# One product of 33 rows for the flags of masked rows, and a start, a router and a weight split that are issued in another order

## The chip, the cores and the metric

One core of one Trainium2 chip. The metric is the device time of one execution in microseconds (us); three runs of the kernel before are shown. TensorE is PE in the views, VectorE is DVE, ScalarE is ACT, GpSimd is POOL, and SP is the engine that only issues transfers (DMAs).

## What is computed

Attention with a bucket mask (a query sees the keys that fall into its own bucket of 64), then a layer that sends each token to the expert with the largest logit, then a two-layer block with a leaky activation, all in float32.

```python
scores = scale * np.matmul(q, k.transpose(0, 1, 3, 2))      # 16 heads, 768 x 768, width 64
scores = np.where(mask, scores, -1000000000.0)              # mask: same bucket
scores = scores - np.max(scores, axis=-1, keepdims=True)
attn = np.exp(scores)
attn = attn / (np.sum(attn, axis=-1, keepdims=True) + 1e-09)
x = np.matmul(attn, v)                                      # 1536 tokens x 512
h = np.maximum(x[tokens] @ w1[e], 0.0)                      # e: the token's expert of 8
y = gate_w * (h @ w2[e])
out = leaky(y @ w_in, alpha) @ w_out
```

A query whose bucket holds no key is a masked row: all its scores are equal, so its output is the mean of v over all keys.

## The kernel before

The 16 heads run as 96 slots, six slots of 128 keys for each head. In slot s PE makes the scores of 128 keys against 768 queries in two halves (ST, L823 and L824), ACT takes the exponential (L825) and its float16 part Eh (L829), POOL the rest El (L830), and four slots later PE multiplies both by v (AV, L838 to L840) into one accumulator `av`, of which there is one. NORM (L851 to L853, DVE) divides it and so frees it for the next head.

A masked row is found from the head's row maxima. MAX (L791 on PE, a reduction at L792 on DVE) computes them some slots ahead of use; POSTb (L797 to L804) transposes them, writes the row `mr` back into the head's operand tile OP by a transfer (L800), which the head's first ST waits for, and compares it with a threshold into the flags `ft`, which a second transfer (L804, for head 0 L814) lays out as one row FL of 768 float16 values. At the end of a head AV adds, for each of six column blocks, flag times total of v, as two products of one row each:

```python
mm(a[:,c*65:c*65+65],fc,VT[:,0,h%4],start=False,stop=False,skip_group_check=True)
mm(a[:,c*65:c*65+64],fc,VT[:,1,h%4,0:64],start=False,stop=(c==5),skip_group_check=True)
```

VT holds the total of v in two float16 parts (high and rest, written by DVE in vtot, L730 and L731). A head's operand tile OP is filled by transfers that SP issues one after another: the bucket bits `zb` (L618 from `big`), A (three transfers) and B (two), which are the float32r part of k and q and its rest; B is made by POOL (L677). `load` (L624, L625) brings k and q of one head.

What is issued when is written by hand: the loop over slots takes its steps in the order of the letters of ORDER, `at`, `sl_at` and `v_at` put a step into a slot, `later` collects transfers for the next flush, and the table PLAN holds slot numbers. `first` there lists the slots whose end runs one more step of the router for the first 768 tokens (some 60 small DVE instructions in all: S, R, star, star2 at L299 to L315, adjust at L324 to L340, its one-hot at L263, GATE at L222 to L228, pre at L350 to L356, gates at L271 to L275). `ga` lists the slots of three gathers of tokens on POOL, and `w1` those of the eight splits of the first expert's weights (L585 on ACT, L588 on DVE). `v0` places the scale of the first v heads: vscale2 (L709 on PE, L711 on DVE) is its last step.

The first microseconds are written out ahead of the loop: WARM idle products of 128x128 (L655), Z0 (bucket bits of heads 0 and 1), six MAX, mrow (L807, L808: the row maxima of head 0 by PE and DVE), six MAX, mrow, then the first ST. `clear` (L653, L654) zeroes one of the five OP tiles on POOL.

Of the kernel before, what the change touches and what calls it, by code (L numbers as in the profile page):

```python
# [9 lines left out]
F32 = mybir.dt.float32  # L10
# [14 lines left out]
NH = 16  # L25
# [11 lines left out]
ORDER = "aVDNmbnefopAL"  # L37
PM = 2
PLAN = dict(
    v0=(1, 2, 4), T3=(2, 2), Z3=(5, 6), T=(2, 4, 5, 7), Z=(8, 10), ld1=5, ld=0, am1=(9, 10, 11, 12), am=(4, 6, 8,  # L40
    10), sc=(13, 15), tot=3, tot0=6, sp=(-2, 4, 10, 18), cap=(3, 2, 0, 1), x=(1, 2, 7, 3), x3=(0, 1, 2, 2), x4=(9, 10, 13, 11), w1=(91, 92, 93, 94, 96, 97, 98, 99), ga=(78, 81, 84), vl=1, am0=(0, 0), Z2=(0, 1), x6=(0, 1, 6, 4), first=(57, 58, 59, 60, 62, 63, 64, 67, 71, 72, 73),
)
NPRE = 3
NT = 22
# [429 lines left out]
def _program(base, tc, nc, q, k, v, proj, mod, w_gate, mbias, w1, w2, win, wout, alpha, out):  # L474
# [142 lines left out]
    def f32(ap): return ap.bitcast(F32)  # L617
# [34 lines left out]
    def clear(i):  # L652
        nc.gpsimd.memset(f32(OP[i][64:128,1:3,:]),0.0)  # L653
        nc.gpsimd.memset(f32(OP[i][96:97,1,:]),1.0)  # L654
    for n in range(WARM): mm(pt[:,128:256],one,one,start=True,stop=True)  # L655
    p0h=ep.tile([128,44],F32R,tag="p0h",name="p0h"); p0l=ep.tile([128,44],F32R,tag="p0l",name="p0l")
    for t in (p0h,p0l): nc.vector.memset(f32(t),0.0)
# [18 lines left out]
        nc.scalar.activation(A[h],raw[h],AF.Copy)  # L676
        nc.gpsimd.tensor_tensor(out=B[h],in0=raw[h],in1=f32(A[h]),op=ALU.subtract)  # L677
    onesh=cp.tile([128,128],F16,tag="onesh",name="onesh")
    VT=cp.tile([1,2,4,65],F16,tag="vt",name="vt")
    FL=[cp.tile([1,768],F16,tag=f"fl{i}",name=f"fl{i}") for i in range(3)]  # L680
    VH=[cp.tile([128,6,4,65],F16,tag=f"vh{i}",name=f"vh{i}") for i in range(2)]
    VL=[cp.tile([128,6,4,64],F16,tag=f"vl{i}",name=f"vl{i}") for i in range(2)]
    DG=[cp.tile([128,4],F32,tag=f"dg{i}",name=f"dg{i}") for i in range(2)]
    def fill():
        for t in DG: nc.gpsimd.memset(t,0.0)
        nc.gpsimd.memset(onesh,2.0**-8)
        nc.gpsimd.memset(VT[:,0,:,64:65],3.0)
# [35 lines left out]
    def vtot(h):  # L723

        w,i=divmod(h,4)
        p=misc()
        for j in range(6):
            mm(p[:,0:64],onesh,VH[w%2][:,j,i,0:64],start=(j==0),stop=False)
            mm(p[:,0:64],onesh,VL[w%2][:,j,i,:],start=False,stop=(j==5))
        nc.vector.tensor_copy(VT[:,0,i,0:64],p[0:1,0:64])  # L730
        nc.vector.tensor_tensor(out=VT[:,1,i,0:64],in0=p[0:1,0:64],in1=VT[:,0,i,0:64],op=ALU.subtract)  # L731

    dq=[];todo=[];now=[True]
    def later(f,p):
        if now[0]: f()
        else: todo.append((p,f))
# [6 lines left out]
    def T(h,half):  # L743
        if half==0:
            half0(h)
        elif h>1:
            OD(h)
            if 4<h+3<NH: at(13,lambda:load(8)) if h==5 else later(lambda:load(h+3),2)
    def OD(h,ns=range(5)):
        t=OP[h%NP]; lo,hi=slice(0,64),slice(64,128)  # L750
        k2=A[h][lo].unsqueeze(1).to_broadcast([64,2,768])
# [25 lines left out]
    def Z0(h,half):  # L777
        p=misc()
        sl=slice(half*384,half*384+384)
        mm(p[0:44,0:384],p0h,A[h][:,sl],start=True,stop=False)  # L780
        mm(p[0:44,0:384],p0h,B[h][:,sl],start=False,stop=False)
        mm(p[0:44,0:384],p0l,A[h][:,sl],start=False,stop=True)
        for o_ in range(2):
            ps=slice(32*o_,32*o_+12)
            nc.vector.tensor_scalar(out=OP[h][64:76,1+o_,sl],in0=p[ps,0:384],scalar1=tv0[ps,0:1],scalar2=tv0[ps,1:2],op0=ALU.is_gt,op1=ALU.mult)
# [7 lines left out]
    def POSTa(h,c0=0,c1=6):  # L793
        nc.vector.tensor_reduce(out=mts[h%2][:,c0:c1],in_=mx[h][:,c0:c1],axis=AX.X,op=ALU.max)
    def POSTb(h,c0=0,c1=6):
        p=misc(); n=c1-c0
        nc.tensor.transpose(p[0:n,0:128],mts[h%2][:,c0:c1],ident)  # L797
        mr=wp.tile([6,128],F32R,tag="mr",name="mr")
        nc.vector.tensor_scalar(out=mr[0:n],in0=p[0:n,0:128],scalar1=MK,scalar2=-1.0,op0=ALU.max,op1=ALU.mult)
        nc.sync.dma_start(out=f32(OP[h%NP][96:97,2,c0*128:c1*128].rearrange("o (c p) -> o c p",p=128)),in_=f32(mr[0:n]))  # L800
        if h not in flT: flT[h]=FL[h%3]
        ft=wp.tile([6,128],F16,tag="ft",name="ft")
        nc.vector.tensor_scalar(out=ft[0:n],in0=p[0:n,0:128],scalar1=MK,scalar2=None,op0=ALU.is_lt)
        later(lambda f=flT[h]:nc.sync.dma_start(out=f[0:1,c0*128:c1*128].rearrange("r (c p) -> r c p",p=128),in_=ft[0:n]),1)  # L804
    def mrow(half):
        p=misc(); hs=slice(half*384,half*384+384)
        for c in range(3): nc.tensor.transpose(p[0:1,c*128:c*128+128],mts[0][:,3*half+c:3*half+c+1],ident)  # L807
        nc.vector.tensor_scalar(out=OP[0][96:97,2,hs],in0=p[0:1,0:384],scalar1=MK,scalar2=-1.0,op0=ALU.max,op1=ALU.mult)  # L808
    def flags0():
        p=misc()  # L810
        nc.tensor.transpose(p[0:6,0:128],mts[0],ident)
        ft=wp.tile([6,128],F16,tag="ft",name="ft"); flT[0]=FL[0]
        nc.vector.tensor_scalar(out=ft,in0=p[0:6,0:128],scalar1=MK,scalar2=None,op0=ALU.is_lt)
        later(lambda:nc.sync.dma_start(out=FL[0][0:1].rearrange("r (c p) -> r c p",p=128),in_=ft),1)  # L814
    E={}
    def ST(s,a):
        h,j=divmod(s,6); t=OP[h%NP]
# [14 lines left out]
    def AV(s):  # L832
        h,j=divmod(s,6); b,hh=divmod(h,8)
        if j==0: av[h]=ps1.tile([128,512],F32,tag="av",name="av")
        _,eh,el=E.pop(s); a=av[h]
        for c in range(6):
            cs=slice(c*128,c*128+128)
            mm(a[:,c*65:c*65+65],eh[:,cs],VH[h//4%2][:,j,h%4,:],start=(j==0 and c==0),stop=False,skip_group_check=True)  # L838
            mm(a[:,c*65:c*65+64],eh[:,cs],VL[h//4%2][:,j,h%4,:],start=False,stop=False,skip_group_check=True)  # L839
            mm(a[:,c*65:c*65+65],el[:,cs],VH[h//4%2][:,j,h%4,:],start=False,stop=False,skip_group_check=True)  # L840
        if j==5:
            for c in range(6):
                fc=flT[h][:,c*128:c*128+128]
                mm(a[:,c*65:c*65+65],fc,VT[:,0,h%4],start=False,stop=False,skip_group_check=True)
                mm(a[:,c*65:c*65+64],fc,VT[:,1,h%4,0:64],start=False,stop=(c==5),skip_group_check=True)
    def NORM(h):
        b,hh=divmod(h,8)
        if hh==0: xs[b]=xsv[b]
# [10 lines left out]
    def at(s,f): other.setdefault(s,[]).append(f)  # L859
    def sl_at(s,f): slot.setdefault(s,[]).append(f)  # L860
# [14 lines left out]
    fill()  # L875
    for u in range(3):
        for a in range(2): MAX(u,a)
    POSTa(0,0,3); mrow(0)
    for u in range(3,6):
        for a in range(2): MAX(u,a)  # L880
    POSTa(0,3,6)
    ahead=(0,1,2)
    Z0(1,0); ST(0,0)
    mrow(1); Z0(1,1); ST(1,0)
    for i in range(2): vam(0,slice(i,i+1))
    ST(2,0)
    direct(2); OD(1,(3,4)); load(3); OD(2,(1,3,4))
    at(1,lambda:load(4)); at(3,lambda:load(5)); sl_at(0,flags0); at(2,lambda:clear(4))
    for i in range(2): at(PLAN["am0"][i],lambda i=i:vam(0,slice(i+2,i+3)))
    for t in range(2): sl_at(PLAN["Z2"][t],lambda t=t:Z((2,),t))  # L890
    v_at(PLAN["v0"][2],0)
# [609 lines left out]
```

## Time and profile before

| what | us |
|---|---|
| median of 3 runs | 712.32 (711.87 to 714.47) |
| the profiled execution | 713.37, its span 711.6 |
| PE busy in the span | 676.3 (95%), 5032 products |
| DVE, ACT, POOL busy | 441.4, 332.9, 234.2 |
| mean granted clock of PE | 0.973 |

The views used below are: the busy time of the engines by stretches, with PE's granted clock (1.00 is 2.4 GHz, 0.50 is 1.2 GHz); the waits of PE; and the timelines of one engine, in which a row gives the start, the time of one instruction or of a merged run (x gives how many), and in brackets the idle time before it with what ended it.

### The profile page before, as it was taken

To read this page: it belongs to the slowest core of one execution; us is meant where nothing else is said; L and a number is where in the kernel's file an instruction comes from. 1 tells how busy PE (TensorE), PEld (TensorE's weight loads), DVE (VectorE), ACT (ScalarE), POOL (GpSimd) and SP (SyncE) were. 2 spreads that over 40 slices of the span, in tenths; PEclk is the share of its full clock that TensorE was granted. 3 is DMA by queue.
4 is the path that set the end of the run, shared out by engine and by line. 5 is a ranking of instruction groups with operands and counts; after the bars stand their busy time and mean duration, and the time that the engine had idled before them with its cause. 6 is when DMAs were issued, how large, how long until landed. Compare 5 with 4: busy or idle time off the path is not lost. (4 is left out here: it accounts for less than half of the span.)

```text
span 711.6 us, 13120 instructions
## 1 busy us (share of the span) xinstructions
PE 676.3 (95%) x5032; PEld 563.1 (79%) x5032; DVE 441.4 (62%) x905; ACT 332.9 (47%) x561; POOL 234.2 (33%) x204
## 2 busy tenths in 40 slices
PE   6789999999899989999999989999999999999996
PEld 5568998998779777788888777788888888888884
DVE  6867888889887668316723557999643344434332
ACT  5556887887677935225524337666311111111111
POOL 8367999898758400210100022021021010110002
PEclk8679999999999999999999999999999999999998
DMA  8267873874625141316622274433011010010001
GB/s 213 70 161 166 179 168 75 179 204 106 136 73 196 41 155 69 105 33 225 220 90 74 81 262 146 134 132 135 1 39 51 0 30 1 15 45 0 1 1 59
DMA packets 31229, 72.40 MB, mean 102 GB/s; under 512 B 6924, under 2 KB 7014, under 8 KB 30902
## 3 DMA queue, kind: packets, MB, share of 16 engines
q1 hardware_dynamic: 28068, 61.78, 30.6%
q0 software_dynamic: 2960, 9.70, 4.0%
q8 instruction: 41, 0.67, 0.4%
q14 instruction: 30, 0.25, 0.1%
q10 hardware_dynamic: 130, 0.00, 0.0%
HBM read 79.15 MB, written 12.06 MB: 128 GB/s over the span
## 5 line engine op out<-in xcount | busy, mean ns | idle before, releaser
L830 POOL TENSOR_TENSOR El<-E,Eh 128x768 f16<-128x768 f32 x88 | 144.3, 1652 | 43.4 <-ACT Eh L829 20.2
L825 ACT ACTIVATE E<-st 128x384 f32<-128x384 f32 x192 | 89.5, 493 | 59.9 <-PE st L824 55.8
L792 DVE TENSOR_REDUCE mx<-mxp 128x1 f32<-128x384 f32 x192 | 97.7, 547 | 10.7 <-PE mxp L791 10.3
L585 ACT ACTIVATE gh<-gf 128x512 fp32r<-128x512 f32 x48 | 30.2, 630 | 143.9 <-PE o L1346 133.4
L829 ACT ACTIVATE Eh<-E 128x768 f16<-128x768 f32 x94 | 79.5, 846 | 0.1
L823 PE MATMUL st<-op 97*128 97x384 f32 x192 | 74.8, 390 | 2.8 <-DMA op<-mr 2.5
L791 PE MATMUL mxp<-op 76*128 76x384 f32 x192 | 68.4, 372 | 5.3 <-DVE mx L792 2.0
L588 DVE TENSOR_TENSOR gl<-gf,gh 128x512 fp32r<-128x512 f32 x48 | 33.1, 690 | 60.0 <-ACT gh L585 57.9
L1048 PE MATMUL y<-op,hh 128*128 128x512 f32 x208 | 69.7, 402 | 0.2 <-DVEq L1257 0.2
L1320 PE MATMUL h<-big,op 128*128 128x512 f32 x256 | 68.5, 396 | 0.0
L824 PE MATMUL st<-op 128*128 128x384 f32 x192 | 67.6, 352 | 0.0
L1363 POOL DMA_INDIRECT out_dram<-x,did x12 | 11.8, 985 | 169.3 <-DVE x L1360 89.8
L1346 PE MATMUL o<-op,gh 128*128 128x512 f32 x192 | 64.2, 395 | 0.0
L1025 PE MATMUL g<-op,xh 128*128 128x512 f32 x192 | 62.6, 397 | 1.3 <-DVEq L1105 0.8
L838 PE MATMUL av<-vh,Eh 128*128 128x65 f16 x576 | 59.7, 198 | 3.7 <-DVE big L853 3.7
L838 PEld LDWEIGHTS <-Eh 128*128 128x128 f16 x576 | 53.1, 99 | 11.4 <-issue 6.8
L839 PE MATMUL av<-vl,Eh 128*128 128x64 f16 x576 | 59.2, 196 | 0.0
L840 PE MATMUL av<-vh,El 128*128 128x65 f16 x576 | 59.0, 196 | 0.0
L1320 PEld LDWEIGHTS h<-big,op 128*128 128x128 f32 x256 | 48.2, 188 | 11.5
L839 PEld LDWEIGHTS <-Eh 128*128 128x128 f16 x576 | 53.9, 100 | 0.1
L840 PEld LDWEIGHTS <-El 128*128 128x128 f16 x576 | 53.8, 99 | 0.0
L1202 POOL DMA_INDIRECT yg<-ys,dpos x10 | 12.4, 1243 | 120.8 <-DVE x L1156 64.6
(404 smaller groups left out, 1510.8 us busy)
## 6 DMA issues: line engine op xcount, KB each, us to landing
r<-in_moe_w_dram SPq DMA_DIRECT2D x42, 1024.0 KB
op<-B SPq DMA_DIRECT2D x32, 192.0 KB
op<-in_moe_w_in_dram SPq DMA_DIRECT2D x6, 1024.0 KB
op<-A SPq DMA_DIRECT2D x28, 192.0 KB
op<-A SPq DMA_DIRECT2D x13, 384.0 KB
op<-in_moe_w_out_dram SPq DMA_DIRECT2D x4, 1024.0 KB
ys<-ysb SPq DMA_DIRECT2D x13, 256.0 KB
big<-in_q_dram SPq DMA_DIRECT2D x17, 192.0 KB
```

The costliest lines, as they stand in the source:

```text
L791: mm(p[:,0:384],t[0:76,2,c*128:(c+1)*128],t[0:76,1,a*384:a*384+384],start=True,stop=True)
L792: nc.vector.tensor_reduce(out=mx[h][:,c,a:a+1],in_=p[:,0:384],axis=AX.X,op=ALU.max)
L823: mm(p[:,0:384],t[0:97,1,js],t[0:97,2,qs],start=True,stop=False)
L824: mm(p[:,0:384],t[:,0,js],t[:,3,qs],start=False,stop=True)
L825: nc.scalar.activation(E[s][0][:,qs],p[:,0:384],AF.Exp,scale=0.125)
L829: else: nc.scalar.activation(eh,e,AF.Copy)
L830: (nc.vector if s>=ELD else nc.gpsimd).tensor_tensor(out=el,in0=e,in1=eh,op=ALU.subtract)
L838: mm(a[:,c*65:c*65+65],eh[:,cs],VH[h//4%2][:,j,h%4,:],start=(j==0 and c==0),stop=False,skip_group_check=True)
L839: mm(a[:,c*65:c*65+64],eh[:,cs],VL[h//4%2][:,j,h%4,:],start=False,stop=False,skip_group_check=True)
L840: mm(a[:,c*65:c*65+65],el[:,cs],VH[h//4%2][:,j,h%4,:],start=False,stop=False,skip_group_check=True)
L1048: nc.tensor.matmul(yps[t], a[:, ks], b[:, kk], start=(kk == 0 and n == 0), stop=(kk == 7 and n == 2))
L1320: nc.tensor.matmul(p, terms[t][0][:, kk, cs], terms[t][1][:, kk], start=(n == 0), stop=(n == 11))
```

## The change

Flags and totals move into one product: VT becomes a tile of 33 rows with the high part of the total in row 0 and the rest in row 32, FL gets 33 rows, cleared once, with the flags in rows 0 and 32. So the flags are transferred twice (32 transfers where there were 16), and AV makes six products per head where it made twelve. In the start, 17 idle products are put in at four places, the loads of heads 4 and 5 are both issued in slot 0 (before: slots 1 and 3), the load of head 6 goes from slot 2's flush to slot 5, the fifth `clear` goes into `fill`, and vscale2 goes from slot 2 to slot 3. In the router star2 goes from slot 62 to 63, adjust from 63 to 71, its one-hot from 64 to 72, GATE from 67 to 75, pre from 71 and 72 to 80 and 81, gates from 73 to 83; the gathers go from slots 78, 81, 84 to 84, 85, 87; six of the eight splits of w1 go two or one slots later.

```diff
-    v0=(1, 2, 4), ...
+    v0=(1, 3, 4), ...
-    ... w1=(91, 92, 93, 94, 96, 97, 98, 99), ga=(78, 81, 84), ... first=(57, 58, 59, 60, 62, 63, 64, 67, 71, 72, 73),
+    ... w1=(91, 92, 95, 96, 97, 98, 99, 100), ga=(84, 85, 87), ... first=(57, 58, 59, 60, 63, 71, 72, 75, 80, 81, 83),
+    def idle(n):
+        p=ps1.tile([128,512],F32,tag="av",name="idle")
+        for _ in range(n): mm(p[:,0:128],one,one,start=True,stop=True)
-    VT=cp.tile([1,2,4,65],F16,tag="vt",name="vt")
-    FL=[cp.tile([1,768],F16,tag=f"fl{i}",name=f"fl{i}") for i in range(3)]
+    VT=cp.tile([33,4,65],F16,tag="vt",name="vt")
+    FL=[cp.tile([33,768],F16,tag=f"fl{i}",name=f"fl{i}") for i in range(3)]
     def fill():
-        nc.gpsimd.memset(VT[:,0,:,64:65],3.0)
+        nc.gpsimd.memset(VT[:,:,64:65],0.0)
+        nc.gpsimd.memset(VT[0:1,:,64:65],3.0)
+        for t in FL: nc.gpsimd.memset(t,0.0)
         clear(3)
+        clear(4)
     def vtot(h):
-        nc.vector.tensor_copy(VT[:,0,i,0:64],p[0:1,0:64])
-        nc.vector.tensor_tensor(out=VT[:,1,i,0:64],in0=p[0:1,0:64],in1=VT[:,0,i,0:64],op=ALU.subtract)
+        nc.vector.tensor_copy(VT[:,i,0:64],p[0:33,0:64])
+        nc.vector.tensor_tensor(out=VT[32:33,i,0:64],in0=p[32:33,0:64],in1=VT[32:33,i,0:64],op=ALU.subtract)
     def T(h,half):
-            if 4<h+3<NH: at(13,lambda:load(8)) if h==5 else later(lambda:load(h+3),2)
+            if 4<h+3<NH: at(13 if h==5 else 5,lambda:load(h+3)) if h in (3,5) else later(lambda:load(h+3),2)
     def POSTb(h,c0=0,c1=6):
-        later(lambda f=flT[h]:nc.sync.dma_start(out=f[0:1,...],in_=ft[0:n]),1)
+        for z in (0,32): later(lambda f=flT[h],z=z:nc.sync.dma_start(out=f[z:z+1,...],in_=ft[0:n]),1)
     def AV(s):
-                mm(a[:,c*65:c*65+65],fc,VT[:,0,h%4],start=False,stop=False,skip_group_check=True)
-                mm(a[:,c*65:c*65+64],fc,VT[:,1,h%4,0:64],start=False,stop=(c==5),skip_group_check=True)
+                mm(a[:,c*65:c*65+65],fc,VT[:,h%4],start=False,stop=(c==5),skip_group_check=True)
-    POSTa(0,0,3); mrow(0)
+    POSTa(0,0,3); idle(7); mrow(0)
     Z0(1,0); ST(0,0)
-    mrow(1); Z0(1,1); ST(1,0)
+    idle(2); mrow(1); idle(3); Z0(1,1); ST(1,0)
-    ST(2,0)
+    ST(2,0); idle(5)
-    at(1,lambda:load(4)); at(3,lambda:load(5)); sl_at(0,flags0); at(2,lambda:clear(4))
+    at(0,lambda:(load(4),load(5))); sl_at(0,flags0)
```

The issue order of SP in slots 0 to 4, where `op_140`, `op_141` and `op_142` are the operand tiles of heads 1, 2 and 3, `big_74` holds raw k and q and the bucket bits, and `fl` the flags. Before:

```order
L814 DMA fl_187<-ft 1x6x128
L624 DMA big_74<-in_k_dram 64x768
L625 DMA big_74<-in_q_dram 64x768
L618 DMA op_141<-big_74 12x768 x2
L618 DMA op_142<-A 64x2x768
L618 DMA op_142<-A 64x768 x2
L618 DMA op_142<-B 64x768 x2
L624 DMA big_74<-in_k_dram 64x768
L625 DMA big_74<-in_q_dram 64x768
L624 DMA big_74<-in_k_dram 64x768
L625 DMA big_74<-in_q_dram 64x768
L800 DMA op_140<-mr 1x6x128
```

And in the change (its line numbers are five or six higher there):

```order
L624 DMA big_74<-in_k_dram 64x768
L625 DMA big_74<-in_q_dram 64x768
L624 DMA big_74<-in_k_dram 64x768
L625 DMA big_74<-in_q_dram 64x768
L820 DMA fl_187<-ft 1x6x128 x2
L618 DMA op_141<-big_74 12x768 x2
L618 DMA op_142<-A 64x2x768
L618 DMA op_142<-A 64x768 x2
L618 DMA op_142<-B 64x768 x2
L806 DMA op_140<-mr 1x6x128
L810 DMA fl_188<-ft 1x6x128 x2
```

Between B of head 3 and `mr` of head 1 no load is left; one load moved ahead of the flags, one behind them.

The order of DVE around the NORM of slot 64 (`r<-av,sc` to `big_73<-av,r`). Before, the second half of adjust stands right ahead of it and the one-hot behind it:

```order
L337 TENSOR_SCALAR misc<-misc 128x6
L338 CAST rq<-misc 128x6
L339 CAST misc<-misc 128x6
L340 CAST rm<-misc 128x6
L851 TENSOR_SCALAR r<-av,sc 128x6
L852 RECIPROCAL r<-r 128x6
L853 TENSOR_TENSOR big_73<-av,r 128x6x64
L792 TENSOR_REDUCE mx<-mxp 128x1 x2
L263 TENSOR_TENSOR big_3223<-iota,misc 128x768
```

In the change star2 stands there, and the maxima follow without the one-hot:

```order
L309 TENSOR_SCALAR misc<-misc,es 128x8
L311 TENSOR_TENSOR so<-misc,iota 128x8
L312 COPY misc<-so 128x8
L315 TENSOR_TENSOR om<-misc,so 128x64
L856 TENSOR_SCALAR r<-av,sc 128x6
L857 RECIPROCAL r<-r 128x6
L858 TENSOR_TENSOR big_73<-av,r 128x6x64
L798 TENSOR_REDUCE mx<-mxp 128x1 x6
```

adjust moved from the slot ahead of this NORM to the slot behind the next one.

The order of PE in the start of the change; before, the three rows of L657 are not there:

```order
L797 MATMUL mxp<-op_139 128x384 x6
L657 MATMUL idle<-one 128x128 x7
L813 MATMUL misc<-ident,mt_181 1x128 x3
L797 MATMUL mxp<-op_139 128x384 x6
L786 MATMUL misc<-A,p0h 44x384
L787 MATMUL misc<-B,p0h 44x384
L788 MATMUL misc<-A,p0l 44x384
L829 MATMUL st<-op_139 128x384
L830 MATMUL st<-op_139 128x384
L657 MATMUL idle<-one 128x128 x2
L813 MATMUL misc<-ident,mt_181 1x128 x3
L657 MATMUL idle<-one 128x128 x3
```

The idle products stand ahead of transposes and products that wait for DVE; five more follow three products of the score, ahead of the maxima of head 1.

## Rows read from the trace of the kernel before

**Rows 1.** Waits of PE from 60 to 150 us: total, times, longest.

```profile
PE mxp L791 <- ACT E L825: 0.7, 1, 0.7
```

**Rows 2.** Timeline of PE at head 0's flags: start, time, product.

```profile
54.17 0.19 PE L839 MATMUL av<-vl,Eh 128*128 128x64 f16 x1
54.20 0.20 PE L840 MATMUL av<-vh,El 128*128 128x65 f16 x1
54.33 0.20 PE L844 MATMUL av<-vt,fl 1*128 1x65 f16 x1
...
54.67 0.19 PE L845 MATMUL av<-vt,fl 1*128 1x64 f16 x1
54.79 0.45 PE L823 MATMUL st<-op 97*128 97x384 f32 x1
```

**Rows 3.** Timeline of PE in the start.

```profile
2.65 4.21 PE L655 MATMUL misc<-one 128*128 128x128 f32 x18 [0.31 <-DVE p0h L657]
...
13.74 0.80 PE L807 MATMUL misc<-ident,mt 128*1 128x128 f32 x3 [1.92 <-DVE mt L794]
...
31.27 0.59 PE L709 MATMUL misc<-dg,one 128*128 128x4 f32 x2 [1.27 <-DVE dg L705]
...
44.36 0.41 PE L823 MATMUL st<-op 97*128 97x384 f32 x1 [2.46 <-DMA op<-mr]
```

**Rows 4.** Stretches: length, busy PE, PEld, DVE, ACT, POOL, clock, DMA share, GB/s.

```profile
10.00:14.00 4.00, 1.78 (x7) 0.97 (x8) 3.52 (x8) 3.32 (x4) 3.80 (x4) 0.58 0.94 209
...
24.00:31.00 7.00, 5.74 (x17) 3.60 (x17) 6.76 (x18) 2.75 (x5) 1.65 (x1) 0.52 0.12 34
31.00:41.00 10.00, 9.73 (x59) 9.23 (x60) 6.96 (x17) 7.12 (x13) 9.47 (x7) 0.50 0.69 172
...
44.00:48.00 4.00, 3.64 (x22) 2.87 (x23) 1.84 (x4) 1.71 (x3) 0.71 (x1) 0.60 0.43 169
```

**Rows 5.** Timeline of SP, 37 to 42 us: start and time of issue.

```profile
37.13 1.10 SPq L618 DMA_DIRECT2D op<-B  x2
...
40.90 0.78 SPq L800 DMA_DIRECT2D op<-mr  x1
41.78 0.73 SPq L804 DMA_DIRECT2D fl<-ft  x1
```

**Rows 6.** Timeline of DVE: the row `mr` of head 1.

```profile
38.26 0.27 DVE L799 TENSOR_SCALAR mr<-misc 6x128 fp32r<-6x128 f32 x1
```

**Rows 7.** Timeline of POOL, 33 to 37 us.

```profile
33.05 1.37 POOL L653 MEMSET op<- 64x1536 f32 x1
...
35.29 1.82 POOL L677 TENSOR_TENSOR B<-big,A 128x768 fp32r<-128x768 f32 x1
```

**Rows 8.** Timeline of DVE around the NORM of slot 64.

```profile
176.38 0.21 DVE L299 TENSOR_SCALAR misc<-k,es 128x8 f32<-128x8 f32 x1
...
179.51 0.16 DVE L324 COPY misc<-e 128x6 f32<-128x6 f32 x1
...
182.28 0.21 DVE L851 TENSOR_SCALAR r<-av,sc 128x6 f32<-128x6 f32 x1
```

**Rows 9.** Timeline of PE: its long waits behind the router's steps.

```profile
183.37 0.20 PE L838 MATMUL av<-vh,Eh 128*128 128x65 f16 x1 [1.93 <-DVE big L853]
...
204.22 0.52 PE L172 MATMUL misc<-ident,big 128*128 128x128 f32 x3 [0.64 <-DVE vt L731]
```

**Rows 10.** The stretch behind the first of these waits, as in rows 4.

```profile
184.00:188.00 4.00, 4.00 (x33) 3.83 (x29) 3.92 (x8) 2.50 (x5) 2.12 (x2) 0.59 1.02 212
```

**Rows 11.** Timelines of DVE and PE near the end of attention.

```profile
248.02 0.67 DVE L588 TENSOR_TENSOR op<-r,op 128x512 fp32r<-128x512 f32 x1
...
249.69 0.24 PE L838 MATMUL av<-vh,Eh 128*128 128x65 f16 x1 [1.76 <-DVE big L853]
```

**Rows 12.** Timelines of SP and PE: `mr` of head 4 and its first product.

```profile
84.47 0.76 SPq L800 DMA_DIRECT2D op<-mr  x1
...
88.97 0.45 PE L823 MATMUL st<-op 97*128 97x384 f32 x1
```

More of the change, by code (lines that the diff above doesn't have):

```diff
@@ L39 @@
 PLAN = dict(
-    v0=(1, 2, 4), T3=(2, 2), Z3=(5, 6), T=(2, 4, 5, 7), Z=(8, 10), ld1=5, ld=0, am1=(9, 10, 11, 12), am=(4, 6, 8,
-    10), sc=(13, 15), tot=3, tot0=6, sp=(-2, 4, 10, 18), cap=(3, 2, 0, 1), x=(1, 2, 7, 3), x3=(0, 1, 2, 2), x4=(9, 10, 13, 11), w1=(91, 92, 93, 94, 96, 97, 98, 99), ga=(78, 81, 84), vl=1, am0=(0, 0), Z2=(0, 1), x6=(0, 1, 6, 4), first=(57, 58, 59, 60, 62, 63, 64, 67, 71, 72, 73),
+    v0=(1, 3, 4), T3=(2, 2), Z3=(5, 6), T=(2, 4, 5, 7), Z=(8, 10), ld1=5, ld=0, am1=(9, 10, 11, 12), am=(4, 6, 8,
+    10), sc=(13, 15), tot=3, tot0=6, sp=(-2, 4, 10, 18), cap=(3, 2, 0, 1), x=(1, 2, 7, 3), x3=(0, 1, 2, 2), x4=(9, 10, 13, 11), w1=(91, 92, 95, 96, 97, 98, 99, 100), ga=(84, 85, 87), vl=1, am0=(0, 0), Z2=(0, 1), x6=(0, 1, 6, 4), first=(57, 58, 59, 60, 63, 71, 72, 75, 80, 81, 83),
 )
@@ L803, in POSTb @@
         nc.vector.tensor_scalar(out=ft[0:n],in0=p[0:n,0:128],scalar1=MK,scalar2=None,op0=ALU.is_lt)
-        later(lambda f=flT[h]:nc.sync.dma_start(out=f[0:1,c0*128:c1*128].rearrange("r (c p) -> r c p",p=128),in_=ft[0:n]),1)
+        for z in (0,32): later(lambda f=flT[h],z=z:nc.sync.dma_start(out=f[z:z+1,c0*128:c1*128].rearrange("r (c p) -> r c p",p=128),in_=ft[0:n]),1)
     def mrow(half):
@@ L813, in flags0 @@
         nc.vector.tensor_scalar(out=ft,in0=p[0:6,0:128],scalar1=MK,scalar2=None,op0=ALU.is_lt)
-        later(lambda:nc.sync.dma_start(out=FL[0][0:1].rearrange("r (c p) -> r c p",p=128),in_=ft),1)
+        for z in (0,32): later(lambda z=z:nc.sync.dma_start(out=FL[0][z:z+1].rearrange("r (c p) -> r c p",p=128),in_=ft),1)
     E={}
```

## The prediction

> **What bounds the kernel now.** First the waits of PE by thirds of the span. From 60 to 150 us PE waits once, 0.7 us [rows 1]: there it is the bound, and a product less is time saved. The start and the stretch behind 164 us are different. The stretches [rows 4] show that the start has two owners: from 24 to 31 us DVE is busy 6.76 of 7 us, and from 31 to 41 us PE is busy 9.73 of 10, but at a granted clock of 0.50, that is 1.2 GHz. Then PE stands for 2.46 us until the row of maxima `mr` of head 1 has landed [rows 3]. Behind 164 us the timelines show DVE as the owner of the two longest waits, 1.93 and 1.76 us, both for the NORM that frees the one accumulator [rows 9, 11]. From 258 us on the order is fixed and PE is busy nearly throughout, so what is gained earlier moves the end.
>
> **The flags.** Twelve products start between 54.33 and 54.67 us, 0.031 us apart, which is also the distance of the products of 128 rows before them (54.17, 54.20) [rows 2]. So six fewer save 0.185 us per head, 2.96 us for 16. Ten heads finish in slots up to 63, where PE is the bound: 1.85 us. Of the six later ones, between waits for DVE, I count half, 0.55. Sum **2.4 us**; ends 1.85 and 2.96. Around the group PE loses time: 0.13 us from the last product before to the first flag, 0.12 from the last flag to the next product, where 0.03 is usual [rows 2], so some 0.19 us per head. No row shows whether 33 rows pay this as one row does; nothing or 3.0 us for 16 heads are the ends, and I count nothing, since the product still fills only part of the array. The Trainium skill, "TensorEngine Tiling", section Key Properties, says that a change of the tiling mode drains the engine; by that rule 33 rows beside 128 keep paying, and the sum stays at 2.4. Without it one could hope for 5.4.
>
> The price of the 33 rows lies elsewhere. DVE's two operations in vtot keep their number and width. POOL gets three clears of 768 float16 values, each at most the 0.73 us of a row of 768 float32 values, hidden in its idle time before the first El. SP gets 16 more issues of about 0.73 us [rows 5]. They stand behind `mr` and ahead of later heads' A and B. The tightest place I found is head 4: `mr` is issued at 84.47 us and, with the 3.46 us from issue to use of head 1 (40.90 to 44.36), usable at 87.93; PE wants it at 88.97 [rows 5, 3, 12]. Two extra issues before that are 1.46 us against 1.04 of slack: 0 to 0.9 us, counted as nothing because SP also waits at times in that stretch.
>
> **The start.** SP issues B of head 3 at 37.13 us, because POOL makes that B only at 35.29, right behind the clear that began at 33.05 [rows 5, 7]. Then come four loads, and `mr`, ready on DVE at 38.53 [rows 6], is issued at 40.90. In the change the clear has gone to POOL's idle time, so B can be done about 2.2 us earlier, and no load is left between B and `mr`. SP waits for DVE alone: `mr` goes at 38.53 instead of 40.90, **2.4 us** earlier, and so does PE's first product of head 1. The load moved behind it is needed only some ten slots later. The two loads moved ahead wait for nothing that is late.
>
> Taking vscale2 out of PE's way removes its 1.27 us [rows 3], but PE then meets the maxima of head 2, whose bits come by a transfer behind DVE's full stretch [rows 4]. So I count nothing for it.
>
> The 17 idle products are to keep the clock up. Nine of their kind took 4.21 us [rows 3], 0.47 each; if that was at half clock, 0.23 at full. The first seven stand in a wait of 1.92 us and at a clock that reads 0.58 [rows 3, 4], so they last 1.6 to 3.3 us: DVE's chain is put off by 0 to 1.4. What follows on DVE is full, so this is not caught up; on the other side the products behind 24 us take half the time if the clock stays up. At best PE gains 2 us more before `mr` and, without a long wait, up to 1.6 in the stretch of 44 to 48 us at 0.60 [rows 4]. So the start is worth 1.0 to 6.0 us, and I take 2.4: the part that hangs on SP and POOL alone.
>
> **The router.** star2 (176.38 to 178.5 us) and adjust (179.51 to 182.28) stand ahead of the NORM of slot 64 [rows 8]. In the change star2 stands in adjust's place: behind the maxima at about 179.2, plus 2.1, the NORM starts at 181.3 instead of 182.28. The wait of 1.93 [rows 9] becomes about 0.95: 1.0 us saved. Behind that wait the clock falls: 184 to 188 us run at 0.59 [rows 10], which costs 4 x 0.41 = 1.6 us. I take it that a wait of half the length does not bring this. Saved: 2.6. adjust, 14 instructions of 0.2 us, now stands in slot 71, where four of pre stood (0.8): DVE is 1.9 us later there, and PE already waits 0.64 us for it [rows 9]. Between nothing and 1.9 us, and 1.6 more if the clock falls, comes back; I take 1.4. GATE, pre and gates move to slots where DVE has idle time, and the gathers have ten slots until their use. Sum **1.2 us**; ends -0.9 and 2.6.
>
> **The splits of w1.** One split stands right ahead of the NORM that ends PE's wait at 249.69, 0.67 us [rows 11]; in the change it is behind. That is 0.7 us, up to 2.1 if the clock, too, does not fall behind the shorter wait. I take **1.1**. The moved splits end up beside and behind the last NORM, where DVE waits for PE.
>
> **The sum.** 2.4 + 2.4 + 1.2 + 1.1 = 7.1 us. The profiled execution took 713.37, so 706.3; it lies 1.05 us above the median of the three runs, so on their scale **705.2 us**.
>
> **The rivals.** *The idle products give back what SP gains.* They run at half clock, DVE's chain is 1.4 us later, and the clock falls again at PE's next wait. The start is worth 1.0 or nothing: 706.6 to 707.6. For it speaks that DVE is full from 24 to 31 us; against it that SP's queue is shorter whatever PE does.
>
> *The stall moves to slot 71.* adjust stops the next accumulator or the maxima for 1.9 us, and the clock falls there: the router gives -0.9 instead of 1.2, 707.3. With the first rival together 709.
>
> *Waits get short and the clock stays at 2.4 GHz*, at 44, 184 and 250 us, or the 0.19 us at the flags' edges go: 3 to 5 us more, about 701.
>
> *The 33 rows do not do what they say*: if a product of 33 rows takes as long as two of one row, the 2.4 us are gone, 707.6. The rows against it: 128 rows are as quick as one.
>
> *SP falls behind, slower.* Each head adds 0.73 us to SP ahead of the next heads' A, B and `mr`. If SP has no idle time left, each of 15 heads' first product comes 0.73 us later, 11 us, and the result is 716.2, slower than before. It decides where `mr` lands behind PE's need, and head 4's slack of 1.04 us is near that point [rows 12]; against it, SP shows idle stretches later, when it waits for DVE.
>
> **How the numbers follow.** About 0.5%, 3.6 us, can be told from no change here: below 708.8 is faster. The forecast as worked out has 0.45, the better case 0.15, the first rival 0.15, the second 0.08, both together or with lost flags 0.09 (708 to 711), the 33 rows alone 0.03, SP 0.05. Faster: 0.45 + 0.15 + 0.15 + 0.08 + 0.03 = 0.86, less 0.05 for the spread of each: 0.81; same 0.14; slower 0.05. For 8 in 10 the range takes the better case and the joint rivals: 700.5 to 709.7.
>
> **What would show it.** Right: 96 products of 33 rows about 0.031 us apart; `mr` of head 1 issued within 0.3 us of its DVE instruction and the wait for it ended near 42 us; the wait at the NORM of slot 64 about 1 us, and the clock behind it 1.00; the last NORM some 6 to 7 us earlier than now and all behind it unchanged. Wrong: long waits for `mr` in later heads (SP), a new wait for DVE in slots 71 to 74, a stretch from 11 to 15 us in which idle products put off the transposes and DVE's next maxima, or a part behind 258 us that does not keep the gain.

## The result, and the profile after

The changed kernel took 708.76 us (median of 20 executions, 705.99 to 711.61), the kernel before in the same rounds 714.50 (20 executions, 711.86 to 721.89). The ratio is 0.9915, 95% interval 0.9898 to 0.9933: 4.8 to 7.3 us less on 714.5. The prediction, 705.2 on 712.32, is a ratio of 0.990; on that scale 0.9915 is 706.3 us. An execution's time goes with PE's mean granted clock, from 705.99 us at 0.991 to 711.61 at 0.982.

The profiled execution of the changed kernel took 711.61 us (span 709.8, clock 0.982) and is the slowest of its 20, while that of before (713.37, clock 0.973) lies below the median of its kernel. So the two traces lie 1.8 us apart where the medians lie 5.7 apart, and a stretch of one trace is one sample. PE is busy 676.0 us, 4970 products.

The timeline of PE in the changed kernel, at the places of [rows 2, 3, 9, 12] (start, time, product, in brackets the idle time before it and what ended it):

```profile
11.62 3.08 PE L657 MATMUL idle<-one 128*128 128x128 f32 x14
...
31.98 0.41 PE L715 MATMUL misc<-dg,one 128*128 128x4 f32 x2 [1.54 <-DVE dg L711]
...
41.67 0.53 PE L829 MATMUL st<-op 97*128 97x384 f32 x1
...
47.79 0.42 PE L797 MATMUL mxp<-op 76*128 76x384 f32 x1 [0.99 <-DMA op<-big]
...
86.66 0.57 PE L829 MATMUL st<-op 97*128 97x384 f32 x1 [1.63 <-DMA op<-mr]
...
147.69 0.20 PE L846 MATMUL av<-vh,El 128*128 128x65 f16 x1
147.82 0.35 PE L850 MATMUL av<-vt,fl 33*128 33x65 f16 x6
148.10 0.44 PE L829 MATMUL st<-op 97*128 97x384 f32 x1
...
179.51 0.44 PE L797 MATMUL mxp<-op 76*128 76x384 f32 x1 [0.49 <-ACT E L831]
...
199.47 0.55 PE L172 MATMUL misc<-ident,big 128*128 128x128 f32 x3 [0.75 <-DVE big L263]
...
238.98 0.20 PE L846 MATMUL av<-vh,El 128*128 128x65 f16 x1 [1.88 <-POOL El L836]
...
253.43 0.50 PE L568 MATMUL g<-op,op 128*128 128x512 f32 x1 [1.63 <-DVE op L558]
```

What is to be seen: the first product of head 1 starts at 41.67 us without a wait (44.36 behind 2.46 us of waiting in [rows 3]). Head 4's now waits 1.63 us for its `mr`; the wait of 0.99 us at 47.79 is for the bucket bits of head 3. The flags' group, from the last product of 128 rows to the next score, takes 0.41 us (147.69 to 148.10), where it took 0.59 in [rows 2]. Both long waits for a NORM [rows 9, 11] are gone, and two new long waits stand near the end of attention, for El on POOL and for the split of x's first group on DVE.

The waits of PE from 60 to 150 us in the changed kernel, which answer to [rows 1] (total, times, longest): the one for `mr` is new.

```profile
PE st L829 <- DMA op<-mr: 1.6, 1, 1.6
PE mxp L797 <- ACT E L831: 0.6, 1, 0.6
PE mxp L797 <- DVE mx L798: 0.2, 1, 0.2
```

The stretches of the changed kernel (columns as in [rows 4]); the first four answer to [rows 4], 184 to 188 us to [rows 10]:

```profile
10.00:14.00 4.00, 3.63 (x17) 3.31 (x18) 3.71 (x8) 3.13 (x4) 3.80 (x4) 0.72 0.94 214
24.00:31.00 7.00, 5.53 (x25) 3.27 (x24) 6.96 (x17) 4.56 (x8) 2.42 (x2) 1.00 0.19 57
31.00:41.00 10.00, 8.37 (x56) 7.26 (x57) 7.19 (x21) 5.89 (x11) 8.40 (x6) 0.56 0.56 126
44.00:48.00 4.00, 3.00 (x50) 2.56 (x47) 2.93 (x8) 3.54 (x7) 2.35 (x2) 1.00 0.60 147
87.00:90.00 3.00, 3.00 (x11) 3.00 (x11) 1.29 (x3) 1.95 (x4) 0.15 (x1) 0.50 0.59 143
184.00:188.00 4.00, 4.00 (x46) 3.44 (x43) 3.42 (x10) 3.55 (x8) 4.00 (x4) 1.00 1.05 213
240.00:244.00 4.00, 4.00 (x37) 3.69 (x36) 3.93 (x8) 2.99 (x6) 0.00 (x0) 0.55 0.03 8
```

The clock holds at 24 to 31 us (1.00 for 0.52), behind the idle products, and at 44 and 184 us too. It falls behind the waits at 31.98, 86.66 and 238.98 us. DVE is as full as before from 24 to 31 us.

The NORMs are marks along the way, each taken here and below at its third instruction (L853 before, L858 in the changed kernel). Of heads 0, 8, 13 and 15 they start at 55.38, 165.64, 235.15 and 257.72 us before, and at 51.82, 164.22, 231.42 and 256.78 in this execution.

### The profile page after: what moved, and what is told of

It is laid out like the page before. It is cut to its first block, busy times and chain, and to the rows that moved or that the text cites. A ratio compares the mean times of both kernels' runs of the same rounds, so it can differ in the third digit from the quotient of the medians.

```text
span 709.8 us, 13037 instructions
## 1 busy us (share of the span) xinstructions
PE 676.0 (95%) x4970; PEld 562.3 (79%) x4970; DVE 443.1 (62%) x905; ACT 331.8 (47%) x561; POOL 237.2 (33%) x208
## 5 line engine op out<-in xcount | busy, mean ns | idle before, releaser
L797 PE MATMUL mxp<-op 76*128 76x384 f32 x192 | 66.3, 359 | 6.9 <-ACT E L831 3.2
```

## The experiments

Each kernel was timed in five rounds beside the kernel before on the same chip; ratios are to before. Not all kernels ran on one chip, so kernels are compared by their ratios. A difference of 1 us between two of them is below what their intervals tell apart, so where a verdict is about less, it rests on the traces.

### The four parts alone

```diff
 flags_only  = before + VT and FL of 33 rows, second flags transfer, one product
 start_only  = before + loads, clear, 17 idle products, vscale2
 router_only = before + first=(57, 58, 59, 60, 63, 71, ...), ga=(84, 85, 87)
 w1_only     = before + w1=(91, 92, 95, 96, 97, 98, 99, 100)
```

Expected of flags_only: 

> Kernel before with the flags' part alone (one product of 33 rows, second transfer of the flags). The sum's theory: 2.4 us less than before (ratio 0.9966), 96 products of 33 rows 0.031 us apart, the loss at the group's edges (0.13 and 0.12 us) as before. Rival, the edges go as well: 5.4 us less (0.9924). Rival, SP: the 16 more issues (0.73 us each) make the row of maxima of head 4 late; before, PE reached it with 1.04 us of slack, so without the earlier start a wait of 0 to 0.9 us stands there and 1.5 to 2.4 us are left (0.9966 to 0.998).

Expected of start_only: 

> Kernel before with the beginning's part alone (loads, clear, 17 idle products, vscale2 one slot later). The changed kernel's trace has PE's first product of head 1 2.7 us earlier than before, then 1.6 us of waiting for the maxima of head 4 and a fall of the clock behind it. Theory, SP and the transfers set head 4 whether or not the flags have a second transfer: the wait for mr of head 4 is here too, above 0.5 us, and 1 to 2 us are left of the start (ratio 0.997 to 0.9985). Rival, the second transfers of the flags of heads 0 to 3 made that wait: no wait for mr of head 4, and the start gives 2.4 to 4 us (0.9945 to 0.9966). Rival of the prediction, the idle products give it all back: 0 to 1 us.

Expected of router_only: 

> Kernel before with the router's lumps and the gathers moved, alone. Theory from the changed kernel's trace: the wait of 1.93 us at the NORM near 183 us goes and with it the clock's fall behind it (2.6 us), some 1.6 us come back in slots 71 to 84 (waits for the one-hot and for E), and the third gather, now right ahead of an El on POOL, makes a wait of about 1.9 us near 240 us with half clock behind it: together between 1 us faster and 2 us slower (ratio 0.9985 to 1.003). Rival, the prediction's sum: 1.2 us faster (0.998) with no wait for El. Rival, the late gather is hidden, since DVE's splits set the end of attention: 2 to 3 us faster (0.996 to 0.997).

Expected of w1_only: 

> Kernel before with five of w1's splits one or two slots later, alone. The sum's theory: 1.1 us faster (0.9985), the wait of 1.76 us for the NORM near 249 us below 1.1 us. Rival from the changed kernel's trace: DVE is full from 239 us to the end of attention, so a split moved behind the NORM comes back as a wait of about 1.6 us at the first product of the expert's first group: no change (0.999 to 1.001). Rival, the clock: without the long wait the products behind it run at full clock, 2 us faster (0.997).

| part | predicted us | ratio | 95% interval | difference of medians, us |
|---|---|---|---|---|
| flags_only | -2.4 | 1.0005 | 0.9984 to 1.0025 | +1.0 |
| start_only | -2.4 | 0.9900 | 0.9869 to 0.9931 | -5.4 |
| router_only | -1.2 | 0.9991 | 0.9965 to 1.0018 | -0.7 |
| w1_only | -1.1 | 0.9990 | 0.9964 to 1.0015 | +0.1 |

The ratio, which is not simply that of the two medians, is the figure with an interval. The beginning's part alone is as fast as the whole change, and gives more than any of the three cases allowed for it; there is no wait for `mr` of head 4 in its trace, so that wait comes with the flags' transfers. The flags' part gives nothing, less than any of its three cases. By the ratios the four parts alone add to 8.1 us, where the whole gave 6.1; the intervals do not tell these apart. The router's ratio lies in the theory's range, with the wait for El near 240 us as expected.

The NORMs tell what stands behind the other two. Router: from head 8 to head 13 it takes 67.31 us (162.94 to 230.25) where before took 69.51, so 2.2 us are saved there, near the 2.6 that the prediction had for the wait and the clock. But from head 13 to head 15 it takes 27.00 us (to 257.25) where before took 22.57: the wait for El, 1.9 us, is in this trace too. The splits of w1 (the edit moves six, where its expectation says five): head 13 to 15 in 21.97 us (236.78 to 258.75), 0.6 less. The wait for the last NORM but one is 1.2 us there (1.76 in [rows 11]). The rival in which the late gather is hidden is out; the sign of either part in the total is not resolved.

### What in the start does it: idle products, or queues

```diff
 start_no_idle = start_only without  idle(7), idle(2), idle(3), idle(5)
 idle_only     = before + idle(7), idle(2), idle(3), idle(5)
```

Expected of start_no_idle: 

> The beginning's part alone, without its 17 idle products (so loads, clear and vscale2 only). The beginning's part with them was 7.1 us faster than before (ratio 0.990). Theory, the clock: the idle products carry most of it, since the stretch of 24 to 31 us ran at 1.00 with them and at 0.50 to 0.57 without; here that stretch is at half clock again and the gain is the 2.4 us that the prediction put on SP and POOL alone, or less (ratio 0.9965 to 1.000). Rival, the queues: the loads and the clear carry it, the idle products only cost time on DVE's chain: 6 us or more faster (0.9915 or below).

Expected of idle_only: 

> Kernel before with the 17 idle products alone: loads, clear and vscale2 as before. The beginning's part without them had a ratio of 0.996, with them 0.990. Theory, the two work in series: the idle products make PE reach the first product of head 1 earlier, but mr of head 1, held by SP and POOL, is issued near 40.9 us as before, so PE only waits longer there: 0 to 1.5 us faster (ratio 0.998 to 1.000) and a wait for mr above 3 us. Rival, the parts add: the clock alone gives the 4 us that separate the two (0.994 to 0.995).

Measured: 0.9960 (0.9941 to 0.9978) without the idle products, 0.9952 (0.9932 to 0.9972) with them alone. So 2.9 and 3.4 us, and both together give 0.9900. Within the intervals the parts add; the theory of work in series was wrong. The stretches of the kernel with the idle products alone, and its first product of head 1:

```profile
24.00:31.00 7.00, 3.89 (x18) 2.15 (x18) 6.89 (x18) 4.00 (x7) 2.84 (x2) 1.00 0.19 55
31.00:41.00 10.00, 9.45 (x54) 8.94 (x55) 7.11 (x18) 6.14 (x11) 9.46 (x8) 0.51 0.82 180
```

```profile
43.36 0.42 PE L826 MATMUL st<-op 97*128 97x384 f32 x1 [1.23 <-DMA op<-mr]
```

And the stretches and the same product with the loads, the clear and vscale2 alone:

```profile
24.00:31.00 7.00, 6.51 (x25) 4.50 (x24) 6.93 (x18) 4.11 (x8) 1.65 (x1) 0.71 0.21 59
31.00:41.00 10.00, 8.00 (x65) 6.49 (x64) 7.74 (x22) 6.84 (x13) 9.93 (x6) 0.83 0.65 138
```

```profile
40.10 0.42 PE L827 MATMUL st<-op 97*128 97x384 f32 x1 [0.34 <-DMA op<-mr]
```

The queues do what the prediction said: `mr` of head 1 is issued 0.3 us behind its DVE instruction, and the product starts at 40.10 us instead of 44.36. The two rows, of DVE and of SP:

```profile
37.17 0.27 DVE L803 TENSOR_SCALAR mr<-misc 6x128 fp32r<-6x128 f32 x1
37.46 0.76 SPq L804 DMA_DIRECT2D op<-mr  x1
```

The idle products work upstream of that: in their trace SP issues B of head 3 at 35.60 us (37.13 in [rows 5]) and `mr` at 39.36 (40.90), with the four loads between them as before. One pair of traces would not show that the clock did this, for router_only, which has no idle products and the start of before, is as early. Its stretch from 24 to 31 us, and its issues of B and `mr`:

```profile
24.00:31.00 7.00, 3.74 (x17) 2.05 (x17) 6.75 (x19) 4.24 (x7) 3.15 (x2) 0.93 0.21 57
```

```profile
35.28 1.10 SPq L618 DMA_DIRECT2D op<-B  x2
...
39.05 0.78 SPq L800 DMA_DIRECT2D op<-mr  x1
```

But its clock was up as well. In the five traces that have the loads and the clear as before, the time from PE's first product of the maxima to the issue of B falls as the clock from 24 to 31 us rises: 28.60 us at 0.50 (w1_only), 27.91 at 0.52 (before), 27.53 at 0.57 (flags_only), 26.55 at 0.93 (router_only) and 26.34 at 1.00 (idle_only). That is the link which the theory in series left out: with PE's clock moves not only PE but what SP waits for. And the idle products keep that clock up: it is 1.00 in all nine traces that have them, and 0.50, 0.52, 0.57, 0.71 and 0.93 in the five that do not. With both, the product starts at 38.83 us.

### What the flags' part takes back

```diff
 no_flags = the change without the flags' part
 act_q    = the change, second flags transfer issued by ACT:
-    nc.sync.dma_start(out=f[z:z+1,...
+    (nc.scalar if z else nc.sync).dma_start(out=f[z:z+1,...
```

Expected of no_flags: 

> The whole change without the flags' part (beginning, router and w1 only). Theory, the flags' part is worth nothing: its six products less per head save 0.14 us each, but the second transfers on SP, the clears ahead of the first scores on POOL and the wait for mr of head 4 take it back: this kernel is as fast as the changed one or faster by up to 2 us (ratio to before 0.9885 to 0.9915), and the 1.6 us wait for mr of head 4 is gone. Rival, the prediction's sum: 2.4 us slower than the changed kernel (0.9945 to 0.995).

Expected of act_q: 

> The whole change with each head's second flags transfer issued from ACT's queue instead of SP's. Theory, SP's issue time makes the flags' part worthless: without 0.73 us per head on SP, mr of heads 1 to 4 is issued as early as in the beginning's part alone, the wait for mr of head 4 falls below 0.8 us, and 1 to 2 us more are gained (ratio to before 0.9885 to 0.990). Rival, the transfer engines, not SP, make mr late (they are busy 0.9 to 1.0 there): the wait stays near 1.6 us and the time is unchanged. Second rival, the issue blocks ACT, which is on the path of the scores: 1 to 5 us slower than the changed kernel.

Measured: 0.9929 (0.9901 to 0.9957) without the flags' part, which leaves the theory and its rival both open by the time alone; 0.9903 (0.9870 to 0.9936) with ACT's queue. The kernel with the flags' part has the lower ratio here, by 1.0 us (0.9915 against 0.9929), and in the pair with a late third gather below by 0.9 (0.9898 against 0.9911); neither is resolved. The traces say more. From head 3's group of flags to head 8's, where PE waits for nothing that matters, before takes 67.05 us and no_flags 67.04, the changed kernel 66.29: 0.15 us per head, predicted 0.185. In 15 heads that is 2.3 us, the size that the prediction had. What it loses again it loses in waits of PE for transfers. For the bits of heads 3 to 5 and `mr` of head 4, PE waits 2.4 to 3.8 us in all in the five traces in which SP issues both flags transfers, 1.2 us in act_q, and 0 to 1.5 us in the eight traces without the flags' part. One pair of traces shows such a loss closely, for up to 43 us all its steps lie 0.2 us apart: no_flags and the change with a late gather (below), which differ there in the flags' part alone. So POOL's clears of FL cost nothing up to there. The issues of SP in no_flags, then in the other:

```profile
37.00 0.71 SPq L808 DMA_DIRECT2D fl<-ft  x1
37.76 0.42 SPq L630 DMA_DIRECT2D vr<-in_v_dram  x1
38.24 0.53 SPq L624 DMA_DIRECT2D big<-in_k_dram  x1
...
41.26 1.63 SPq L618 DMA_DIRECT2D op<-big  x2
```

```profile
37.19 1.44 SPq L810 DMA_DIRECT2D fl<-ft  x2
38.69 0.43 SPq L630 DMA_DIRECT2D vr<-in_v_dram  x1
39.17 0.53 SPq L624 DMA_DIRECT2D big<-in_k_dram  x1
...
41.41 1.63 SPq L618 DMA_DIRECT2D op<-big  x2
```

PE's wait for those bits of head 3 in no_flags, then in the other, with the stretch behind it:

```profile
44.79 0.41 PE L795 MATMUL mxp<-op 76*128 76x384 f32 x1 [1.23 <-DMA op<-big]
```

```profile
45.76 0.41 PE L797 MATMUL mxp<-op 76*128 76x384 f32 x1 [2.04 <-DMA op<-big]
```

```profile
47.00:50.00 3.00, 3.00 (x34) 2.70 (x33) 2.25 (x6) 2.49 (x5) 2.58 (x3) 0.50 1.00 239
```

The bits are issued at nearly the same time (41.26 and 41.41), but the load of head 6 stands 0.93 us later ahead of them, the product that needs the bits starts 0.97 us later, the wait is 0.8 us longer, and behind the longer wait the clock is 0.50 from 47 to 50 us; behind the shorter one it held at 1.00. Head 0's group of flags starts at 47.94 and 50.43 us: less the 0.2, one more issue of 0.7 us has become 2.3. That the bits queue behind the load fits the other traces of this start: from their issue to their use it is 4.35 us where the load began 2.2 us ahead of them (late_gather), 3.3 to 3.6 where it began 2.9 to 3.5 ahead (six traces), and 3.23 where it was moved away (load6_11 and load6_9, below).

Where PE waits differs from one execution to the next. In the changed kernel's own trace the bits cost 0.99 us and the clock held behind them; there the loss stands at `mr` of head 4, as the prediction had feared. From head 2's flags to head 3's it takes 16.18 us, 13.39 with the late gather: 2.8 us, for the wait of 1.63 and the clock of 0.50 from 87 to 90 us. DVE had that `mr` ready some 3.5 us before SP, with A, B and a load ahead of it, came to issue it:

```profile
77.64 0.27 DVE L805 TENSOR_SCALAR mr<-misc 6x128 fp32r<-6x128 f32 x1
```

```profile
81.43 0.76 SPq L806 DMA_DIRECT2D op<-mr  x1
```

ACT's queue did not free this. In act_q the second transfer of head 4's flags, 1.5 KB, was issued by ACT at 76.71 us, and SP's issue of `mr` waited 4.3 us for it, until 82.92, with the transfer engines at 1.02 to 1.06 from 76 to 82 us; PE waited 1.19 us for that `mr`. The row of SP's waits:

```profile
SPq L806 <- DMA fl<-ft: 4.3, 1, 4.3
```

Such a wait stands in no trace in which SP issues both transfers; it came with the edit. So this run shows that a small transfer of another queue is slow as well while the engines are full, but it does not tell SP's issue time from the transfers: in the changed kernel's trace both hold `mr` up, 3.5 us before its issue and 5.2 from issue to use (81.43 to 86.66). The Trainium skill, "DMA: Bandwidth & Descriptors", section "Issuing engines are not separate DMA queues", says that transfers run on the same 16 engines whoever starts them; the 6.2 us of ACT's 1.5 KB agree with it.

### The third gather behind POOL's last El

```diff
-    ga=(84, 85, 87)
+    ga=(84, 85, 91)
 late_gather   = the change with this
 no_flags_late = no_flags with this
```

Expected of late_gather: 

> The whole change with the third gather in slot 91 instead of 87, behind POOL's last El; PE's, DVE's, ACT's and SP's orders are those of the changed kernel. Theory: the wait of 1.88 us for El at 239 us goes, the clock does not fall behind it, and since DVE owns the end of attention half of that stays: 1 to 3 us faster than the changed kernel (ratio to before 0.9873 to 0.990). Rival: DVE, full from 239 us on, sets the end whatever PE does, and nothing changes (0.9905 to 0.9925).

Expected of no_flags_late: 

> The change without the flags' part, with the third gather in slot 91. Theory, the late third gather made the wait of 1.9 us for El and the half clock behind it in any version: this kernel is 1.5 to 3 us faster than the one without flags (0.9929), so 0.9887 to 0.991, level with the late gather alone, which has the flags' part. Rival, the flags' part does save 2.4 us when nothing waits for SP: this kernel is 2 us slower than the late gather alone (0.9925 to 0.994).

In the changed kernel's trace the timeline of POOL shows what the El waited for:

```profile
235.75 1.51 POOL L612 DMA_INDIRECT big<-x_d,idp  x1 [0.16 <-issue]
237.27 1.65 POOL L836 TENSOR_TENSOR El<-E,Eh 128x768 f16<-128x768 f32 x1
```

With the gather behind it, in the timeline of PE of late_gather:

```profile
234.32 0.20 PE L846 MATMUL av<-vh,El 128*128 128x65 f16 x1 [0.18 <-POOL El L836]
```

The wait of 1.88 us is 0.18, and the 1.63 us for the split of x are gone. But the clock still falls, which the theory did not expect, only later and behind a shorter wait, for DVE. In late_gather, that wait and the stretch behind it:

```profile
240.56 0.83 PE L186 MATMUL misc<-wg,big 128*128 128x8 f32 x6 [0.68 <-DVE lg L190]
```

```profile
242.00:248.00 6.00, 5.32 (x74) 4.75 (x73) 5.85 (x13) 3.67 (x7) 0.00 (x0) 0.50 0.01 3
```

From head 13's NORM to head 15's it takes 23.32 us (228.48 to 251.80) for 25.36 in the changed kernel, and 22.71 for 25.63 without the flags: 2.0 and 2.9 us in the traces, in the theory's range. Measured: 0.9898 (0.9872 to 0.9923) and 0.9911 (0.9880 to 0.9941). Against 0.9915 and 0.9929 both went the expected way, by 1.2 and 1.3 us, and neither step is resolved by its interval.

### The load of head 6 out of the way of the bits

```diff
-            if 4<h+3<NH: at(13 if h==5 else 5,lambda:load(h+3)) if h in (3,5) else ...
+            if 4<h+3<NH: at(13 if h==5 else 11,lambda:load(h+3)) if h in (3,5) else ...
 load6_11 = late_gather with this; load6_9: 9 for 11
```

Expected of load6_11: 

> The whole change with the third gather in slot 91 and the load of head 6 in slot 11 instead of 5, so behind the bits of head 3 on SP. In the trace of the changed kernel with the late gather the load was issued at 39.17 us, 0.9 us later than without the second flags transfer, the bits of head 3 landed at 45.7 instead of 44.7, PE waited 2.04 us for them instead of 1.23, and the clock fell to 0.50 from 47 to 50 us. Theory: without the load ahead of them the bits land 1 to 2.5 us earlier, the wait falls below 1.2 us, the clock holds, and the first NORM starts 1.5 to 3 us earlier than at 51.3: 1.5 to 3 us faster than the late gather alone (ratio to before 0.9855 to 0.988). Rival: the load, moved ahead of head 4's bits, only puts the wait off to head 4: no change (0.989 to 0.9905).

Expected of load6_9: 

> As the run with the load of head 6 in slot 11, but in slot 9. In slot 11 the load was issued at 57.24 us, right ahead of the four transfers of bits of heads 4 and 5 (59.01), and PE waited 2.43 us for those, with the clock at 0.50 to 0.59 from 62 to 68 us. In slot 9 it stands at about 52.4 us, where the transfer engines were at 0.47. Theory: the bits of head 3 are as early as in slot 11 (wait of 0.9 us or less instead of 2.04), those of heads 4 and 5 have no wait above 0.5 us, and the clock holds at both places: the NORM of head 1 starts by 66 us (66.8 with the late gather alone, 70.0 in slot 11), and the run is 1 to 3 us faster than the late gather alone (ratio to before 0.9855 to 0.9885). Rival: SP is full, and the load's two issues make A and B of head 4 and then the maxima of head 2, 3 or 4 late; a wait of more than 1 us stands at one of them and nothing is gained (0.989 to 0.993).

Measured: 0.9926 (0.9898 to 0.9953) and 0.9942 (0.9917 to 0.9966): nothing gained, as the rivals had it, and both a little above the rivals' ranges. In both, head 3's bits cost 0.9 us instead of 2.04, and head 0's NORM starts at 49.89 and 49.66 us instead of 51.31; but PE's next wait is for those of heads 4 and 5, in load6_11 and in load6_9:

```profile
62.82 0.66 PE L797 MATMUL mxp<-op 76*128 76x384 f32 x1 [2.43 <-DMA op<-big]
```

```profile
62.18 0.42 PE L797 MATMUL mxp<-op 76*128 76x384 f32 x1 [2.02 <-DMA op<-big]
```

Head 3's NORM starts at 95.59 and 93.20 us, at 92.93 with the load where it was, at 96.25 in the changed kernel, and at 90.69 and 90.79 in the two without the flags' part. Of these only the last two and late_gather met the same clock in the start (1.00 from 10 to 14 us, see the last section), so 2.1 to 2.2 us is what these traces say of the second transfers. In the traces of the two moves, each time PE comes earlier, the next transfer is late; whether another place for the load avoids that, no run shows.

No version tried is shown to beat the changed kernel. The late gather has the lowest ratio, 0.9898 to 0.9915, with intervals that overlap.

## Why the prediction was right, and where not

**The time** was right: 705.2 on 712.32 against a ratio of 0.9915, and faster by more than 0.5%. But the four terms, 2.4, 2.4, 1.2 and 1.1, are not what makes it: the beginning's part alone gives 0.990. Errors of opposite sign cancelled, the start too low and the other three too high, and that they did is luck. The sign "the last NORM some 6 to 7 us earlier" cannot be read from the two traces shown (257.72 and 256.78), since the changed kernel's is its slowest execution.

**The flags, 2.4 predicted, nothing measured alone (0.9984 to 1.0025), about 1 us, not resolved, within the change.** The count was right: 96 products of 33 rows about 0.03 us apart, 0.15 us per head. The edges stay, as the prediction counted them: 0.13 us from the last product of 128 rows to the first flag (147.69 to 147.82), as in [rows 2]. The Trainium skill, "TensorEngine Tiling (Array Packing)", section Key Properties, says that a change of the tiling mode drains the engine; gaps that stay with 33 rows agree with it, but no run shows that they are this drain. The failed sentence is "0 to 0.9 us, counted as nothing because SP also waits at times in that stretch". I had looked for a late `mr` of head 4, and it came: 1.63 us of wait in the profiled execution, for the 0 to 0.9 that the prediction worked out, and the clock fell behind it, which the prediction had not priced: 2.8 us. The same loss can stand 40 us earlier, at the bits of head 3, a transfer that I had not followed: in late_gather, behind the second flags transfer, come the load of head 6 and then the bits, and 2.3 us are lost there. In flags_only the two kinds of wait, 1.5 us for bits and 0.9 us for `mr` of head 4, are there as well.

**The start, 2.4 predicted, 5.4 measured by the medians, 7.1 by the ratio.** "The part that hangs on SP and POOL alone" was sized rightly: 2.9 us without the idle products. In the changed kernel, too, `mr` of head 1 is issued 0.30 us behind its DVE instruction (38.15 behind 37.85). The failed step is the zero for the 17 idle products: they give 3.4 us alone. The prediction had this gain in its better case, as PE time up to `mr`; that DVE, POOL and SP come earlier with PE was missing. Its opposite, the put-off chain on DVE, is real in some executions: where the first seven ran at a clock of 0.72 they took 3.08 us, in start_only at 1.00 they took 1.72. What this does to DVE's chain shows in DVE's wait for the transposes behind them, before, in the changed kernel and in start_only:

```profile
14.57 0.55 DVE L808 TENSOR_SCALAR op<-misc 1x384 fp32r<-1x384 f32 x1 [0.98 <-PE misc L807]
```

```profile
15.35 0.55 DVE L814 TENSOR_SCALAR op<-misc 1x384 fp32r<-1x384 f32 x1 [1.54 <-PE misc L813]
```

```profile
14.00 0.55 DVE L812 TENSOR_SCALAR op<-misc 1x384 fp32r<-1x384 f32 x1 [0.67 <-PE misc L811]
```

The wait is 0.98 us in all five traces without idle products, 1.25 to 1.54 in the five whose start met the lower clock, and 0.67 in the four that met 1.00. So the chain is put off by 0.3 to 0.6 us or comes 0.3 earlier, where I gave 0 to 1.4 later.

**The router, 1.2 predicted, 0.7 measured and not resolved.** The wait at the NORM of slot 64 and the clock behind it went, further than said: no wait for this NORM is left, the longest behind it is 0.49 us, 184 to 188 us run at 1.00, and in router_only 2.2 us are saved by head 13. (The sum had the NORM start 2.1 us behind 179.2; [rows 8] show 179.51, so by these rows it was 0.7 us, not 1.0.) In slot 71 the wait is 0.75 us at 199.47, where it was 0.64 [rows 9]: 0.1 us came back there, far below the 1.4 taken. The failed sentence is "the gathers have ten slots until their use": true of their data, but each takes 1.0 to 1.5 us of POOL, and the third now stands right ahead of an El that PE wants. I had counted the users of a moved instruction and not the queue that it stands in. That cost 1.88 us of waiting, and the clock was 0.55 from 240 to 244 us behind it. With the gather out of the way the clock still fell there, later and for another wait, so not all of this is the gather's.

**The splits of w1, 1.1 predicted, 0.6 in the trace, not resolved in the time.** The wait of 1.76 us at the NORM was shortened to 1.2, not removed, in w1_only.

**The rivals.** SP falling behind was no slowdown of 11 us, but its mechanism, small transfers late at the point where PE has become early, is what took the flags' gain. The better case, waits short and the clock kept, came in the start, from 24 to 31 us, and at 184 us; at 240 us it failed, in the change behind the gather and in late_gather without it. The stretch behind 258 us kept what it was given: from the last NORM to the end of the span 453.9 us before and 453.0 in the changed kernel.

## What to carry to other kernels

A product less where PE is the bound was worth its distance here only where no transfer that feeds PE came late for it; follow every transfer behind an added one, and look at small rows and bits that queue behind large loads. When an instruction is moved, price the queue at its new place as well as the wait at its old one. Where the start runs at half clock while other engines wait for PE, idle products in PE's own waits can be worth as much as a repaired queue (3.4 and 2.9 us here).

## What the runs showed of the hardware that was not expected

The same start met two clocks. In nine profiled executions with the 17 idle products, the first seven of them met a clock of 1.00 from 10 to 14 us in four (start_only, late_gather, no_flags, no_flags_late) and 0.59 to 0.76 in five (the changed kernel 0.72, act_q 0.76, idle_only 0.59, load6_11 0.65, load6_9 0.60), though PE's order up to that point is the same. The four are also 0.3 to 0.6 us earlier at PE's first product of the maxima (8.79 to 8.99 us for 9.26 to 9.43), ahead of any idle product. Between the changed kernel and start_only DVE's first row of maxima lies 1.35 us apart, of which 0.47 stands ahead of the idle products and 0.87 is the longer wait behind them.

How long the last wait was does not tell what the clock does behind it. A wait of 1.54 us (at 31.98 in the changed kernel) was followed by half clock to some 42 us (0.56 over 31 to 41 us), one of 1.53 us at the same product of late_gather (30.64) by 0.83 over 31 to 41 us. One of 1.23 us (44.79 in no_flags) was followed by no fall, 2.04 us at the same place by half clock from 47 to 50 us, and one of only 0.68 us (240.56 in late_gather) by half clock from 242 to 248 us.

A transfer of 1.5 KB took some 6 us from ACT's issue to SP's release (76.71 to 82.92) while the engines' share was 1.02 to 1.06 up to 82 us, with A and B in front of it; in the changed kernel a row of 3 KB took 5.2 us from issue to use (81.43 to 86.66).
